# Attention, a PReLU layer pair and an expert mixture on one core: the second layer of ten expert pairs as seven block products, with the split weights kept in DRAM

## The chip, the cores and the metric

The kernel runs on 1 core of one Trainium2 chip. The metric is the device time of one execution in microseconds (us). Before the change the median of 3 runs is 849.52 us (847.73 to 849.97). The engines are TensorE (PE; its weight loads are listed apart as PEld), VectorE (DVE), ScalarE (ACT), GpSimd (POOL) and SyncE (SP), which only issues DMAs here.

## The reference, cut to what matters

```
attn = attention(q, k, v)             # local window of 16 plus block summaries; 2 x 8 heads x 768 x 64
x    = attn as 1536 tokens x 512
h    = x @ w_in                       # 512 x 2048
x    = (max(h, 0) + alpha * min(h, 0)) @ w_out
p    = domain_probs / (domain_probs.sum(-1) + 1e-9)
out  = 0
for e in range(4):                    # w1[e]: 512 x 1024, w2[e]: 1024 x 512
    h    = max(x @ w1[e], 0)
    out += p[:, e:e+1] * (h @ w2[e])
```

All of it is float32. The two batches of 768 tokens are worked on one after the other in the expert stage.

## The kernel before, in words

PE multiplies in the format fp32r. To keep float32 accuracy each operand is split into a high part (an ACT copy to fp32r) and a low part (a subtraction, value minus high part), and each product is three matmuls that add up in PSUM: high x high, high x low, low x high. Each matmul has its own weight load of 128 x 128.

The first two fifths of the span are attention and the PReLU layer, by an order written out by hand (`ORDER`) and then by unit (the loop over `units`). The expert stage follows (lines 726 to 749). It has 32 steps s: batch b = s // 16 and pair q = s % 16. A pair is 256 of the 4096 hidden columns, so four pairs make one expert.

*First layer of a step.* The 512 x 256 weight block and the 512 x 768 operand of a batch are cut into 2 x 2 blocks (256 x 128 of the weights, 256 x 384 tokens of the operand) and multiplied by seven block products instead of eight (Strassen's scheme in Winograd's form): `p1` to `p7` in `e_steps` (544). Each is 6 matmuls of 384 columns (2 row blocks x 3 terms). Results are combined by ACT copies (`keep`) and DVE sums, and `result` makes the high part `gh` (ACT, with the Relu) and the low part `gl` (DVE) of the hidden values. The sums of weights (S1 to S4) come from POOL (`e_sums`, 384), those of the operand (T1 to T4) from DVE (`x_combine`, 505).

*Second layer of a step.* `l2b` (612) takes six token tiles of 128. For each, 6 matmuls of 512 columns (2 row blocks x 3 terms) fill one PSUM bank, and DVE adds the bank, times the token's probability, to the accumulator `acc2`. The second layer of step s is carried out in step s + 1. The last tile of all goes in two halves of 256 columns (`l2b_last`, 596).

*Weights.* `e_prep(s)` (394) makes the split weights of step s, one step ahead. The raw weights come by DMA from SP into three slots tagged `raw`: `ra` for the first layer, `rb` for the second. ACT makes high parts and POOL low parts (`e_split`, 377), into rings of seven buffers. Both batches do this, so each pair is loaded and split twice.

*Order.* In the expert stage the order on PE and ACT is that of the program text (`manual_schedule`, 726): `p1`, the `p4` of the step before, `p2`, `p6`, the `p3` of the step before, `p5`, `p7`, and then the six `l2b` tiles with the pieces of `e_prep(s + 1)` merged in between. DVE, POOL and SP get their order from a planner that simulates the program. Each engine then takes its instructions strictly in order. In the steps 10 to 14 one piece each of the second batch's operand splits (`own1`) is merged in, in step 15 `late1`, in step 16 `last1`.

Of the kernel before, what the change touches and what calls it, by code (L numbers as in the profile page):

```python
# [16 lines left out]
B, H, S, D = 2, 8, 768, 64  # L17
P = 128
# [6 lines left out]
NAC = S // P  # L25
DM = H * D
KD = DM // P
FF1 = 2048
NE = 4
# [3 lines left out]
NFB = NF1 + NF2  # L33
G = 4
WBUFS = 7
MBUFS = 5
NG1 = NF1 // G
NQ = NF2 // 2
TP = S // 2
C0 = 256  # L40
CH = 512
NT = B * S // P

# [48 lines left out]
def kernel(  # L92
# [202 lines left out]
    ws, pw = {}, {}  # L295
# [74 lines left out]

    def e_load_b(s):
        q = s % NQ
        t = wp.tile([P, 2, DM], F32, tag="raw", name="rb", bufs=3)
        nc.sync.dma_start(out=t, in_=wb_in[1, 2 * q:2 * q + 2].rearrange("i p n -> p i n"))
        pw["b", s] = t

    def e_split(pool, k, src, n=DM):
        hi = pool.tile([P, n], F32R, tag="h", name=f"w{k}h")
        lo = pool.tile([P, n], F32R, tag="l", name=f"w{k}l")
        nc.scalar.activation(hi, src, AF.Copy)  # L380
        nc.gpsimd.tensor_tensor(lo, src, hi.bitcast(F32), op=ALU.subtract)  # L381
        return hi, lo

    def e_sums(s):
# [6 lines left out]
        nc.gpsimd.tensor_tensor(s34[:, 1], r[:, 2], s12[:, 1], op=ALU.subtract)  # L391
        pw["s", s] = s12, s34

    def e_prep(s):
        if s >= 2 * NQ:
            return []

        def part(names, src, pool=wpool[0]):
            hi, lo = e_split(pool, 0, src, len(names) * 2 * P)
            for i, name in enumerate(names):  # L400
                ws[s, name] = hi[:, i * 2 * P:(i + 1) * 2 * P], lo[:, i * 2 * P:(i + 1) * 2 * P]

        def flat(t):
            return t.rearrange("p a c -> p (a c)")

        steps = [
            lambda: part(("A11", "A12"), flat(pw["a", s][:, 1:3])),
            lambda: e_sums(s),
            lambda: part(("S1", "S2"), flat(pw["s", s][0])),
            lambda: part(("S3", "S4"), flat(pw["s", s][1])),  # L410
            lambda: part(("A22",), pw["a", s][:, 3], wa22),
        ]
        if s + 1 < 2 * NQ:
            steps.append(lambda: e_load_a(s + 1))
        for i in range(2):
            steps.append(lambda i=i: ws.__setitem__((s, i), e_split(wpool[1], 1, pw["b", s][:, i])))
        if s + 1 < 2 * NQ:
            steps.append(lambda: e_load_b(s + 1))
        return steps


    gs = {}
# [110 lines left out]
    def product(ps, s, b, aname, bname, first):  # L533
# [5 lines left out]
        for i, (l, r) in enumerate(terms):  # L539
            nc.tensor.matmul(  # L540
                ps, l, r, start=(first and i == 0), stop=(i == len(terms) - 1), skip_group_check=True
            )

    def e_steps(s):
        b = s // NQ
        v = {}

        def keep(name, ps):
            v[name] = gp.tile([P, TP], F32, tag="m", name=name, bufs=MBUFS)
            nc.scalar.activation(v[name], ps, AF.Copy)  # L550

        def result(f, half, src):
            gh = gp.tile([P, TP], F32R, tag="gh", name="gh")
            gl = gp.tile([P, TP], F32R, tag="gl", name="gl")
            gs[s, f, half] = gh, gl
            nc.scalar.activation(gh, src, AF.Relu)
            nc.vector.scalar_tensor_tensor(gl, src, 0.0, gh.bitcast(F32), op0=ALU.max, op1=ALU.subtract)

        def p1():
            v["b"] = ps_1.tile([P, TP], F32, tag="l1", name="cb")  # L560
            product(v["b"], s, b, "A11", "B11", True)
            keep("p1", v["b"])

        def p2():
            a = ps_w.tile([P, TP], F32, tag="w", name="ca")
            product(a, s, b, "A12", "B21", True)
            nc.vector.tensor_tensor(a, a, v["p1"], op=ALU.add)
            result(0, 0, a)

        def p6():  # L570
            product(v["b"], s, b, "S2", "T2", False)
            keep("u2", v["b"])

        def p5():
            v["d"] = ps_1.tile([P, TP], F32, tag="l1", name="cd")
            product(v["d"], s, b, "S1", "T1", True)

        def p7():
            product(v["b"], s, b, "S3", "T3", False)
            keep("u3", v["b"])  # L580
# [12 lines left out]

        return [p1, p2, p6, p5, p7, p4, p3]

    def l2b_last(s, i):

# [95 lines left out]
    for p in range(4 * G, 4 * G + 3):  # L693
        w_load(p)
    first.close()
    xe = ctx.enter_context(tc.tile_pool(name="xe", bufs=1))
    xeh = xe.tile([P, 3, 2, TP], F32R, name="xeh")
    xel = xe.tile([P, 3, 2, TP], F32R, name="xel")
    wa22 = ctx.enter_context(tc.tile_pool(name="wa22", bufs=2))
    ps_w = ctx.enter_context(tc.tile_pool(name="ps_w", bufs=2, space=PSUM))  # L700

    gp = ctx.enter_context(tc.tile_pool(name="gb", bufs=6))
    mbufs = MBUFS
    for f in (l1_minus, l1_prelu, l1_high, l1_low):
        f(G, 0, CH)
    for u, (n, c0, size) in enumerate(units):
# [17 lines left out]


    with tc.manual_schedule(engines={mybir.EngineType.PE, mybir.EngineType.Activation}):
        left = []
        l2 = l2_steps(len(units) - 1)[KD // 2:]
        for s in range(2 * NQ):
            p1, p2, p6, p5, p7, p4, p3 = e_steps(s)  # L730
            for f in [p1] + left[:1] + [p2, p6] + left[1:] + [p5, p7]:
                f()
            side = e_prep(s + 1)
            if NQ - 1 - len(own1) <= s < NQ - 1:
                side = side[:3] + [own1[s - NQ + 1 + len(own1)]] + side[3:]
            elif s == NQ - 1:
                side = late1 + side
            elif s == NQ:
                side = last1 + side
            keep = l2[-1:] if s == 2 * NQ - 1 else []  # L740
            merge(l2[:len(l2) - len(keep)], side)
            left = [p4, p3]
            l2 = [lambda i=i, s=s: l2b(s, i) for i in range(NAC)]
        for f in left + keep + l2[:-1]:
            f()
        l2b_last(2 * NQ - 1, NAC - 1)
# [59 lines left out]
```

## Time and profile before

| | |
|---|---|
| time of the runs | 849.52 us median, 847.73 to 849.97 |
| time of the profiled execution | 849.81 us |
| its span, first to last instruction | 848.0 us |
| granted TensorE clock, mean | 0.996 of full speed |
| DMA | 76.61 MB, mean 90 GB/s |
| HBM read / written | 72.63 MB / 3.15 MB |

The page of the profile gives the busy time of each engine, the chain of work that ended last, groups of instructions with their mean time, and DMA issues. A PE busy for 97% is not PE at its peak, since a matmul's duration in the records (0.39 us for 512 columns) is longer than the distance to the next start. So matmuls are read by their starts.

### The profile page before, as it was taken

To read this page: it belongs to the slowest core of one execution; us is meant where nothing else is said; L and a number is where in the kernel's file an instruction comes from. 1 tells how busy PE (TensorE), PEld (TensorE's weight loads), DVE (VectorE), ACT (ScalarE), POOL (GpSimd) and SP (SyncE) were. 2 spreads that over 40 slices of the span, in tenths; PEclk is the share of its full clock that TensorE was granted. 3 is DMA by queue.
4 is the path that set the end of the run, shared out by engine and by line. 5 is a ranking of instruction groups with operands and counts; after the bars stand their busy time and mean duration, and the time that the engine had idled before them with its cause. 6 is when DMAs were issued, how large, how long until landed. Compare 5 with 4: busy or idle time off the path is not lost.

```text
span 848.0 us, 12730 instructions
## 1 busy us (share of the span) xinstructions
PE 824.3 (97%) x4622; PEld 734.9 (87%) x4622; DVE 548.1 (65%) x1144; ACT 401.4 (47%) x988; POOL 326.8 (39%) x326
## 2 busy tenths in 40 slices
PE   4799999999999999999999999999999999999998
PEld 3689999888888888989889898898899899898997
DVE  7998767999983447455555576856555555545555
ACT  4999995544432324443433434534534434344340
POOL 0000000000022200475675676765766756756630
PEclk9899999999999999999999999999999999999999
DMA  8999412333320000113122122122322131121201
GB/s 303 286 307 295 147 44 76 100 99 100 100 75 25 26 1 0 50 51 100 51 67 83 50 73 77 50 77 72 125 84 66 50 99 51 57 93 50 75 1 75
DMA packets 39695, 76.61 MB, mean 90 GB/s; under 512 B 3792, under 2 KB 15568, under 8 KB 39632
## 3 DMA queue, kind: packets, MB, share of 16 engines
q1 hardware_dynamic: 39056, 75.51, 28.2%
q8 instruction: 36, 0.59, 0.3%
q10 hardware_dynamic: 576, 0.28, 0.1%
q14 instruction: 27, 0.22, 0.1%
HBM read 72.63 MB, written 3.15 MB: 89 GB/s over the span
## 4 chain that ended last, share of the span: by engine, by line
PE 86%; DVE 7%; DMA 3%; ACT 2%; issue 0%; SPq 0%; ACTq 0%
PE l L428 58%; PE cb L540 15%; PE cd L540 7%; PE ca L540 4%; DVE acc L519 1%; DVE acc L626 1%; DMA vcat<-in_vw 1%; PE s L212 1%; PE xps L274 1%; ACT sm L231 1%; DVE sm L222 1%; DMA kv<-in_vt 1%; DVE vs L176 1%; DMA raw<-in_wa 1%; PE pt L256 1%; DMA mask<-in_mask 1%
## 5 line engine op out<-in xcount | busy, mean ns | idle before, releaser
L381 POOL TENSOR_TENSOR w0l<-ra,w0h 128x512 fp32r<-128x512 f32 (+1 forms) x64 | 70.4, 1100 | 349.9 <-ACT w0h L380 349.9
L626 DVE SCALAR_TENSOR_TENSOR acc<-l,prob_sb,acc 128x512 f32<-128x512 f32 x179 | 133.8, 750 | 74.6 <-PE l L428 74.6
L428 PE MATMUL l<-w1h,gh 128*128 128x512 f32 (+1 forms) x386 | 149.8, 388 | 1.1 <-DVE acc L626 1.1
L428 PE MATMUL l<-w1h,gl 128*128 128x512 f32 (+1 forms) x386 | 150.4, 390 | 0.0
L428 PE MATMUL l<-w1l,gh 128*128 128x512 f32 (+1 forms) x386 | 150.3, 389 | 0.0
L381 POOL TENSOR_TENSOR w0l<-s,w0h 128x512 fp32r<-128x512 f32 x64 | 85.6, 1357 | 2.9 <-ACT w0h L380 2.9
L381 POOL TENSOR_TENSOR w1l<-rb,w1h 128x512 fp32r<-128x512 f32 x64 | 81.9, 1301 | 11.9 <-ACT w1h L380 11.9
L428 PEld LDWEIGHTS l<-w1h,gh 128*128 128x128 f32 x386 | 72.5, 188 | 15.8 <-DVE acc L626 1.6
L428 PEld LDWEIGHTS l<-w1h,gl 128*128 128x128 f32 x386 | 72.4, 188 | 15.0
L428 PEld LDWEIGHTS l<-w1l,gh 128*128 128x128 f32 x386 | 72.4, 188 | 14.4
L428 PE MATMUL l<-xh,w0h 128*128 128x512 f32 (+1 forms) x240 | 84.5, 352 | 0.0
L428 PE MATMUL l<-gh,w1h 128*128 128x512 f32 (+1 forms) x240 | 83.3, 350 | 0.0
L428 PE MATMUL l<-xl,w0h 128*128 128x512 f32 (+1 forms) x240 | 83.1, 346 | 0.0
L428 PE MATMUL l<-xh,w0l 128*128 128x512 f32 (+1 forms) x240 | 83.1, 346 | 0.0
L428 PE MATMUL l<-gh,w1l 128*128 128x512 f32 (+1 forms) x240 | 82.9, 347 | 0.0
L550 ACT ACTIVATE p<-cb 128x384 f32<-128x384 f32 x32 | 15.7, 492 | 140.3 <-PE cb L540 140.3
L428 PE MATMUL l<-gl,w1h 128*128 128x512 f32 (+1 forms) x240 | 81.4, 347 | 0.0
L388 POOL TENSOR_TENSOR s<-ra 128x256 f32<-128x256 f32 x32 | 23.6, 738 | 125.6 <-DMA ra<-in_wb 121.7
L540 PE MATMUL cb<-xeh,w0h 128*128 128x384 f32 x192 | 64.4, 335 | 0.2
L540 PE MATMUL cb<-xeh,w0l 128*128 128x384 f32 x192 | 64.2, 334 | 0.0
L540 PE MATMUL cb<-xel,w0h 128*128 128x384 f32 x192 | 64.2, 334 | 0.0
L453 DVE SCALAR_TENSOR_TENSOR l<-m,beta,l 128x512 f32<-128x512 f32 (+1 forms) x60 | 38.6, 644 | 23.8 <-ACT m L447 23.7
(104 smaller groups left out, 1836.4 us busy)
## 6 DMA issues: line engine op xcount, KB each, us to landing
raw<-in_wa SPq DMA_DIRECT2D x32, 512.0 KB, 3.8
ra<-in_wb SPq DMA_DIRECT2D x64, 256.0 KB, 3.0
rb<-in_wb SPq DMA_DIRECT2D x32, 512.0 KB, 3.6
q<-in_qh SPq DMA_DIRECT2D x24, 256.0 KB, 5.3
kw<-in_kw SPq DMA_DIRECT2D x24, 192.0 KB, 5.5
vcat<-in_vw SPq DMA_DIRECT2D x12, 384.0 KB, 6.3
kv<-in_kt SPq DMA_DIRECT2D x8, 384.0 KB, 5.7
kv<-in_vt SPq DMA_DIRECT2D x8, 384.0 KB, 6.0
```

The lines of the kernel that those rows point to most:

```text
L176: nc.vector.tensor_reduce(vs[:, hp, KW:NK], st.pop(("v", b, hp)), axis=AX.X, op=ALU.add)
L212: nc.tensor.matmul(sp[:, u], q[:, u // 2, u % 2], kw[:, :, u // 2, u % 2], start=True, stop=True)
L222: nc.vector.tensor_tensor_reduce(sm[:, u], sp[:, u], mask[:, m], -1.0 / math.sqrt(D), 3.0e38, ALU.add, ALU.min, mx[:, u:u + 1],)
L231: nc.scalar.activation(sm[:, u], sm[:, u], AF.Exp, bias=mx[:, u:u + 1], scale=-1.0, accum_out=sume[:, u:u + 1],)
L256: nc.tensor.transpose(pt[0:NK, u], pp[:, u], ident)
L381: nc.gpsimd.tensor_tensor(lo, src, hi.bitcast(F32), op=ALU.subtract)
L388: nc.gpsimd.tensor_tensor(s12[:, 0], r[:, 0], r[:, 3], op=ALU.add)
L428: ins = nc.tensor.matmul(ps, a, c, start=(i == 0), stop=(i == n - 1))
L453: nc.vector.scalar_tensor_tensor(ps, m, beta[:, i:i + 1], ps, op0=ALU.mult, op1=ALU.add)
L540: nc.tensor.matmul(ps, l, r, start=(first and i == 0), stop=(i == len(terms) - 1), skip_group_check=True)
L550: nc.scalar.activation(v[name], ps, AF.Copy)
L626: nc.vector.scalar_tensor_tensor(acc2[:, t], ps, pe, acc2[:, t], op0=ALU.mult, op1=ALU.add)
```

## The change

- For the five pairs of steps (18, 19) to (26, 27), all in the second batch, the second layers of two steps are done together. 768 tokens x 512 hidden columns times 512 x 512 weights are cut into 2 x 2 blocks, and seven block products take the place of eight (`l2_quad`). Each is 3 token tiles x 6 matmuls of 256 columns. DVE adds each finished half bank to one or two blocks of the accumulator. These products are mixed into the first-layer products of the following steps by a pattern (`paired`), in which a dot stands for one group of 6 matmuls.
- The sums of hidden values that this needs are made on DVE (`s_sums`), from float32 copies of the Relu results that ACT writes (`field`), and split by ACT and POOL (`s_split`).
- The sums of weights (T1 to T4) for these pairs are made on DVE in the first batch (`t_sums`), split by ACT and DVE (`t_split`) and written to DRAM.
- In the first batch every split weight is also written to DRAM (`put`). In the second batch nothing is split any more; the parts are read back (`e_fetch`, `b_load`).
- `rb` of odd steps gets a buffer of its own; the ring of first-layer copies shrinks from 5 to 4; the operand splits of the second batch (`own1`) move to steps 12 to 14.

```diff
-MBUFS = 5
+MBUFS = 4
+UA, UB = NQ + 2, 2 * NQ - 4
...
     def e_load_b(s):
         q = s % NQ
-        t = wp.tile([P, 2, DM], F32, tag="raw", name="rb", bufs=3)
+        if s % 2:
+            t = gp.tile([P, 2, DM], F32, tag="rb", name="rb", bufs=1)
+        else:
+            t = wp.tile([P, 2, DM], F32, tag="raw", name="rb", bufs=3)
...
+    def put(dst, pair):
+        for h, t in enumerate(pair):
+            nc.sync.dma_start(out=dst[:, h], in_=t.bitcast(F32))
...
+    def t_place(i):
+        k, c = 2 * (i % 2), S + 2 * P * (1 + i // 2)
+        return slice(None), slice(k, k + 2), slice(c, c + 2 * P)
+
+    def t_view(s, i):
+        d = 2 * P * (i in (1, 2))
+        return pw["b", s - i % 2][:, :, d:d + 2 * P]
+
+    def t_sums(s):
+        t1, t2, t3, t4 = (t_view(s, i) for i in range(4))
+        for y, p, q in ((t1, t3, t1), (t3, t2, t3), (t2, t2, t1), (t4, t4, t2)):
+            nc.vector.tensor_tensor(y, p, q, op=ALU.subtract)
+
+    def t_split(s, i):
+        t, hi, lo = t_view(s, i), xh[t_place(i)], xl[t_place(i)]
+        nc.scalar.activation(hi, t, AF.Copy)
+        nc.vector.tensor_tensor(lo, t, hi.bitcast(F32), op=ALU.subtract)
+        put(dt[unit(s), i], (hi, lo))
...
     def e_prep(s):
         if s >= 2 * NQ:
             return []
+        if s >= NQ:
+            return [lambda: e_fetch(s)]
 
         def part(names, src, pool=wpool[0]):
...
+            pair = e_split(pool, 0, src, len(names) * 2 * P)
+            named(s, names, *pair)
+            put(da[s, names[0]], pair)
+
+        def second(i):
+            ws[s, i] = e_split(wpool[1], 1, pw["b", s][:, i])
+            put(dw[s, i], ws[s, i])
...
+        if s % 2 and quad(s + NQ):
+            steps.append(lambda: t_sums(s))
+        elif s % 2 == 0 and quad(s - 1 + NQ):
+            for i in range(4):
+                steps.insert(2 * i + 1, lambda i=i: t_split(s - 1, i))
         return steps
...
         def result(f, half, src):
+            if quad(s):
+                name = f"A{half + 1}{2 - s % 2}"
+                if name == "A21":
+                    nc.scalar.activation(field(s, name, f), src, AF.Relu)
+                    return
...
+            if quad(s):
+                nc.scalar.activation(field(s, name, f), src, AF.Relu)
...
+    def s_sums(s, f):
+        a11, a12, a21, a22 = (field(s, n, f) for n in ("A11", "A12", "A21", "A22"))
+        nc.vector.tensor_tensor(a22, a21, a22, op=ALU.add)
+        nc.vector.tensor_tensor(a21, a11, a21, op=ALU.subtract)
+        nc.vector.tensor_tensor(a11, a22, a11, op=ALU.subtract)
+        nc.vector.tensor_tensor(a12, a12, a11, op=ALU.subtract)
+
+    def s_split(s, k, f):
+        src, c = field(s, ("A22", "A11", "A12", "A21")[k], f), slice(f * TP, (f + 1) * TP)
+        nc.scalar.activation(xh[:, k, c], src, AF.Copy)
+        nc.gpsimd.tensor_tensor(xl[:, k, c], src, xh[:, k, c].bitcast(F32), op=ALU.subtract)
+
+    def l2_quad(a):
...
+        plan = (
+            ("B21", base(a, 0), 0, True, ((0, 0),)),
+            ("T4", base(a, 1), 1, True, ((1, 0),)),
+            ("B11", base(a + 1, 0), 0, True, ((0, 0),)),
+            ("T1", summed(0), 1, False, ((1, 1),)),
+            ("T2", summed(1), 0, False, ((0, 1),)),
+            ("B22", summed(2), 1, False, ((0, 1),)),
+            ("T3", summed(3), 0, False, ((1, 0), (1, 1))),
+        )
+
+        def go(k, i):
...
+            ps = u[i][:, part]
+            (bh, bl), terms = bs[n, bname], []
+            for f in range(2):
+                gh, gl = left(f, 0, i), left(f, 1, i)
+                terms += [(gh, bh[:, f]), (gh, bl[:, f]), (gl, bh[:, f])]
...
+            for half, d in to:
+                t = NAC + half * (NAC // 2) + i
+                dst = acc2[:, t, d * 2 * P:(d + 1) * 2 * P]
+                nc.vector.scalar_tensor_tensor(dst, ps, prob_sb[:, t, e:e + 1], dst, op0=ALU.mult, op1=ALU.add)
+            if i == NAC // 2 - 1 and a + 2 < UB:
+                b_load(n + 1, bname)
...
+        own_at = {NQ - 4: own1[:2], NQ - 3: own1[2:4], NQ - 2: own1[4:], NQ - 1: late1, NQ: last1}
...
+                paired(a, "1.2.6.5.7..4.3" if n == 7 else "1.2.6..5.7..4..3.", old[done:13], splits)
+                paired(a + 1, "1.2..6..5.7..4..3.", old[13:] + q[:3])
...
+        paired(UB, "1..2..6...5..7...4...3...", old[done:], splits)
```

## Rows read from the trace of the kernel before

**Rows 1.** The page, busy us, share of the span, instructions of each engine:
```profile
PE 824.3 (97%) x4622; PEld 734.9 (87%) x4622; DVE 548.1 (65%) x1144; ACT 401.4 (47%) x988; POOL 326.8 (39%) x326
```

**Rows 2.** Waits of PE, 300 us to the end: us in total, times, longest:
```profile
PE l L428 <- DVE acc L626: 1.1, 1, 1.1
```

**Rows 3.** Windows by step: us, then busy time per engine, clock, DMA share, GB/s:
```profile
451.19:466.70 15.51, 15.51 (x80) 14.06 (x79) 8.29 (x13) 6.28 (x13) 9.99 (x10) 1.00 0.22 69
...
497.71:513.88 16.17, 16.05 (x80) 13.97 (x79) 13.90 (x18) 7.02 (x14) 10.83 (x10) 1.00 0.21 65
545.59:561.09 15.50, 15.50 (x79) 14.05 (x79) 9.36 (x15) 6.69 (x14) 10.84 (x12) 1.00 0.22 69
576.60:593.55 16.95, 15.80 (x79) 13.98 (x79) 11.89 (x17) 7.94 (x17) 9.92 (x11) 1.00 0.18 62
```

**Rows 4.** The chain of waits, one step: start us, us, what:
```profile
609.06 8.20 PE l L428 x36
617.26 2.10 PE cb L540 x12
624.57 8.20 PE l L428 x36
```

**Rows 5.** Timeline of PE at the end: start us, us, engine, line, operation:
```profile
843.14 0.28 PE L428 MATMUL l<-w1h,gh 128*128 128x256 f32 x1
...
844.45 0.28 PE L428 MATMUL l<-w1h,gl 128*128 128x256 f32 x1
```

**Rows 6.** The chain of waits in the first stage, 125 to 127 us:
```profile
125.28 2.04 PE l L428 x17
```

**Rows 7.** Groups of DVE, whole span: count | busy us, mean ns | idle before:
```profile
L626 DVE SCALAR_TENSOR_TENSOR acc<-l,prob_sb,acc 128x512 f32<-128x512 f32 x179 | 133.8, 750 | 74.6 <-PE l L428 74.6
...
L341 DVE TENSOR_TENSOR t<-t,e 128x512 f32<-128x512 f32 x32 | 21.7, 682 | 0.1
...
L591 DVE TENSOR_TENSOR cd<-cd,u 128x384 f32<-128x384 f32 x32 | 18.1, 566 | 9.9 <-PE cd L540 9.9
...
L609 DVE SCALAR_TENSOR_TENSOR acc<-l,prob_sb,acc 128x256 f32<-128x256 f32 x2 | 1.0, 483 | 0.2 <-PE l L428 0.2
```

**Rows 8.** Groups of ACT and of POOL, 600 to 800 us:
```profile
L380 ACT ACTIVATE w1h<-rb 128x512 fp32r<-128x512 f32 x26 | 14.8, 615 | 0.0
...
L556 ACT ACTIVATE gh<-cd 128x384 fp32r<-128x384 f32 x13 | 6.4, 491 | 15.7 <-DVE cd L591 15.7
...
L381 POOL TENSOR_TENSOR w0l<-ra,w0h 128x512 fp32r<-128x512 f32 x13 | 19.0, 1460 | 18.1 <-ACT w0h L380 18.1
...
L381 POOL TENSOR_TENSOR w0l<-ra,w0h 128x256 fp32r<-128x256 f32 x13 | 9.6, 739 | 0.0
```

**Rows 9.** Timelines of DVE and of POOL, 576 to 594 us:
```profile
579.16 1.02 DVE L501 TENSOR_TENSOR xel<-acc,xeh 128x384 fp32r<-128x384 f32 x2
...
580.76 3.11 DVE L501 TENSOR_TENSOR xel<-acc,xeh 128x384 fp32r<-128x384 f32 x2
...
580.59 1.30 POOL L381 TENSOR_TENSOR w0l<-ra,w0h 128x512 fp32r<-128x512 f32 x1 [3.05 <-ACT w0h L380]
```

**Rows 10.** Timeline of POOL, end of one step's work and its gap:
```profile
458.15 2.54 POOL L381 TENSOR_TENSOR w1l<-rb,w1h 128x512 fp32r<-128x512 f32 x2
464.56 0.74 POOL L388 TENSOR_TENSOR s<-ra 128x256 f32<-128x256 f32 x1 [3.87 <-DMA ra<-in_wb]
```

**Rows 11.** Windows of attention's loads and of the last output writes, columns as above:
```profile
20.00:60.00 40.00, 34.67 (x319) 30.80 (x320) 38.60 (x157) 38.11 (x142) 0.00 (x0) 0.91 1.00 308
...
838.00:844.00 6.00, 6.00 (x32) 5.10 (x31) 3.56 (x5) 0.00 (x0) 0.00 (x0) 1.00 0.41 158
```

**Rows 12.** Timeline of SP's queue, one load of raw weights:
```profile
445.23 0.34 SPq L367 DMA_DIRECT2D ra<-in_wb  x1
445.61 0.56 SPq L368 DMA_DIRECT2D ra<-in_wb  x1
```

More of the change, by code (lines that the diff above doesn't have):

```diff
@@ L392, in e_sums, with quad, unit, get @@
         pw["s", s] = s12, s34
+    def quad(s):
+        return UA <= s < UB
+    def unit(s):
+        return (s - UA % NQ) // 2
+    def put(dst, pair):
+        for h, t in enumerate(pair):
+            nc.sync.dma_start(out=dst[:, h], in_=t.bitcast(F32))
+    def get(pool, src, n=DM):
+        hi = pool.tile([P, n], F32R, tag="h", name="wfh")
+        lo = pool.tile([P, n], F32R, tag="l", name="wfl")
+        for h, t in enumerate((hi, lo)):
+            nc.sync.dma_start(out=t.bitcast(F32), in_=src(h))
+        return hi, lo
@@ new lines, in b_load @@
+    def b_load(j, name):
+        half = slice(0, 2 * P) if name in ("B11", "B21") else slice(2 * P, DM)
+        hi = wpool[1].tile([P, 2, 2 * P], F32R, tag="h", name="bh")
+        lo = wpool[1].tile([P, 2, 2 * P], F32R, tag="l", name="bl")
+        for h, t in enumerate((hi, lo)):
+            if name[0] == "T":
+                nc.sync.dma_start(out=t.bitcast(F32), in_=dt[j, int(name[1]) - 1][:, h])
+            else:
+                for f in range(2):
+                    a = UA % NQ + 2 * j + 2 - int(name[1])
+                    nc.sync.dma_start(out=t[:, f].bitcast(F32), in_=dw[a, f][:, h, half])
+        bs[j, name] = hi, lo
@@ new lines, with named, e_fetch @@
+    PARTS = (("A11", "A12"), ("S1", "S2"), ("S3", "S4"), ("A22",))
+    def named(s, names, hi, lo):
+        for i, name in enumerate(names):
+            ws[s, name] = hi[:, i * 2 * P:(i + 1) * 2 * P], lo[:, i * 2 * P:(i + 1) * 2 * P]
+    def e_fetch(s):
+        q = s % NQ
+        for names in PARTS:
+            n = len(names) * 2 * P
+            pool = wpool[0] if len(names) > 1 else wa22
+            named(s, names, *get(pool, lambda h: da[q, names[0]][:, h], n))
+        if not quad(s):
+            for f in range(2):
+                ws[s, f] = get(wpool[1], lambda h: dw[q, f][:, h])
@@ L396, in e_prep @@
             return []
+        if s >= NQ:
+            return [lambda: e_fetch(s)]
         def part(names, src, pool=wpool[0]):
-            hi, lo = e_split(pool, 0, src, len(names) * 2 * P)
-            for i, name in enumerate(names):
-                ws[s, name] = hi[:, i * 2 * P:(i + 1) * 2 * P], lo[:, i * 2 * P:(i + 1) * 2 * P]
+            pair = e_split(pool, 0, src, len(names) * 2 * P)
[4 more added lines that the diff above has]
+            put(dw[s, i], ws[s, i])
         def flat(t):
@@ L412, in e_prep @@
         ]
-        if s + 1 < 2 * NQ:
+        if s + 1 < NQ:
             steps.append(lambda: e_load_a(s + 1))
         for i in range(2):
-            steps.append(lambda i=i: ws.__setitem__((s, i), e_split(wpool[1], 1, pw["b", s][:, i])))
-        if s + 1 < 2 * NQ:
+            steps.append(lambda i=i: second(i))
+        if s + 1 < NQ:
             steps.append(lambda: e_load_b(s + 1))
+        if s % 2 and quad(s + NQ):
[3 more added lines that the diff above has]
+                steps.insert(2 * i + 1, lambda i=i: t_split(s - 1, i))
         return steps
@@ L542, in product, with field @@
             )
+    bs, fs = {}, {}
+    def field(s, name, f):
+        if name == "A12":
+            j = (s - UA) // 2
+            if (j, name) not in fs:
+                fs[j, name] = wp.tile([P, 2, TP], F32, tag="raw", name="a12", bufs=3)
+            return fs[j, name][:, f]
+        k = 2 * ("A22", "A11", "A21").index(name) + f
+        return acc[:, k * TP:(k + 1) * TP]
     def e_steps(s):
@@ new lines, in l2_quad, with base, summed @@
+    def l2_quad(a):
+        n, u = (a - UA) // 2, {}
+        def base(s, half):
+            return lambda f, h, i: gs[s, f, half][h][:, i * P:(i + 1) * P]
+        def summed(k):
+            return lambda f, h, i: (xh, xl)[h][:, k, f * TP + i * P:f * TP + (i + 1) * P]
+        plan = (
[8 more added lines that the diff above has]
+        def go(k, i):
+            bname, left, part, first, to = plan[k]
+            if k == 0:
+                u[i] = ps_2.tile([P, 2, 2 * P], F32, tag="l2", name="l2q")
+            ps = u[i][:, part]
+            (bh, bl), terms = bs[n, bname], []
+            for f in range(2):
+                gh, gl = left(f, 0, i), left(f, 1, i)
+                terms += [(gh, bh[:, f]), (gh, bl[:, f]), (gl, bh[:, f])]
+            for j, (l, r) in enumerate(terms):
+                nc.tensor.matmul(
+                    ps, l, r, start=(first and j == 0), stop=(j == len(terms) - 1), skip_group_check=True
+                )
+            e = a % NQ * NE // NQ
+            for half, d in to:
[4 more added lines that the diff above has]
+                b_load(n + 1, bname)
+        return [lambda k=k, i=i: go(k, i) for k in range(len(plan)) for i in range(NAC // 2)]
@@ L695 @@
     first.close()
+    dr = ctx.enter_context(tc.tile_pool(name="dr", bufs=1, space=bass.MemoryType.DRAM))
+    da, dw, dt = {}, {}, {}
+    for q in range(NQ):
+        for names in PARTS:
+            da[q, names[0]] = dr.tile([P, 2, len(names) * 2 * P], F32, name=f"da{q}{names[0]}")
+        for f in range(2):
+            dw[q, f] = dr.tile([P, 2, DM], F32, name=f"dw{q}{f}")
+    for j in range((UB - UA) // 2):
+        for i in range(4):
+            dt[j, i] = dr.tile([P, 2, 2, 2 * P], F32, name=f"dt{j}{i}")
     xe = ctx.enter_context(tc.tile_pool(name="xe", bufs=1))
@@ L726, with standard @@
     with tc.manual_schedule(engines={mybir.EngineType.PE, mybir.EngineType.Activation}):
-        left = []
+        left, keep = [], []
         l2 = l2_steps(len(units) - 1)[KD // 2:]
-        for s in range(2 * NQ):
+        own_at = {NQ - 4: own1[:2], NQ - 3: own1[2:4], NQ - 2: own1[4:], NQ - 1: late1, NQ: last1}
+        def standard(s, l2, left):
             p1, p2, p6, p5, p7, p4, p3 = e_steps(s)
+            if not left:
+                left, l2 = l2[:2], l2[2:]
             for f in [p1] + left[:1] + [p2, p6] + left[1:] + [p5, p7]:
@@ L733 @@
             side = e_prep(s + 1)
[L734 to L739, printed above, removed]
+            if s in own_at:
+                side = side[:3] + own_at[s] + side[3:]
             keep = l2[-1:] if s == 2 * NQ - 1 else []
             merge(l2[:len(l2) - len(keep)], side)
-            left = [p4, p3]
@@ L743, with paired @@
-            l2 = [lambda i=i, s=s: l2b(s, i) for i in range(NAC)]
+            return [lambda i=i, s=s: l2b(s, i) for i in range(NAC)], [p4, p3], keep
+        def paired(s, order, fill, after=()):
+            fill, after = iter(fill), iter(after)
+            steps = dict(zip("1265743", e_steps(s)))
+            e_prep(s + 1)[0]()
+            for x in order:
+                if x == ".":
+                    next(fill)()
+                    next(after, lambda: None)()
+                    continue
+                steps[x]()
+                if s % 2 and quad(s) and x in "43":
+                    s_sums(s, int(x == "4"))
@@ new lines @@
+        for s in range(UA):
+            l2, left, _ = standard(s, l2, left)
+        for name in ("B21", "T4", "B11"):
+            b_load(0, name)
+        old = None
+        for a in range(UA, UB, 2):
+            q = l2_quad(a)
+            if old is None:
+                paired(a, "1.26.57...4...3", left + l2)
+                for name in ("T1", "T2", "B22", "T3"):
+                    b_load(0, name)
+                paired(a + 1, "1.2.6.57..4.3", q[:6])
+                k = 6
+            else:
+                splits = [lambda k=k, f=f, s=a - 1: s_split(s, k, f) for k in range(4) for f in (1, 0)][1:]
+                n = 13 - done
+                paired(a, "1.2.6.5.7..4.3" if n == 7 else "1.2.6..5.7..4..3.", old[done:13], splits)
+                paired(a + 1, "1.2..6..5.7..4..3.", old[13:] + q[:3])
+                k = 3
+            s_split(a + 1, 0, 1)
+            old, done = q, k
@@ L744 @@
+        splits = [lambda k=k, f=f, s=UB - 1: s_split(s, k, f) for k in range(4) for f in (1, 0)][1:]
+        paired(UB, "1..2..6...5..7...4...3...", old[done:], splits)
+        l2, left = [lambda i=i: l2b(UB, i) for i in range(NAC)], []
+        for s in range(UB + 1, 2 * NQ):
+            l2, left, keep = standard(s, l2, left)
         for f in left + keep + l2[:-1]:
```

## The prediction, made before the changed kernel was run

> **What bounds the kernel now.** I read the busy shares first. PE (TensorE) is busy for 97% of the span, the next engine, DVE, for 65%, and ACT and POOL for less than half [rows 1]. The list of waits says the same of the stretch this change touches: from 300 us to the end PE waited once, for 1.1 us [rows 2]. So only two things move the time here: the columns that PE has to stream, and new waits of PE.
>
> Then I cut the expert stage into its 32 steps by time. An undisturbed step takes 15.50 to 15.51 us with PE busy throughout, DVE 8.29, ACT 6.28 and POOL about 10 [rows 3]. The chain of waits shows what a step consists of: 36 second-layer matmuls of 512 columns in 8.20 us, and until the next such block 7.31 us for the 42 product matmuls of 384 columns, the first twelve in 2.10 [rows 4]. That is 0.228 and 0.174 us each. Twelve second-layer matmuls of 256 columns stand at the very end: from the first start to the last, 843.14 to 844.45, are 11 spacings of 0.119 us [rows 5]; seventeen in the first stage take 2.04 us, 0.120 each [rows 6]. Their weight loads of 0.19 us overlap and do not set this spacing. I take 0.1195 us.
>
> **Part 1, PE columns.** Ten steps (18 to 27) become five pairs. Before, a pair's second layer is 72 matmuls x 0.228 = 16.40 us. After, it is 7 products x 3 token tiles x 2 row blocks x 3 terms = 126 matmuls of 256 columns, 126 x 0.1195 = 15.06 us. The saving is 1.34 us a pair, 6.7 us for five. The first-layer products are unchanged. An eighth fewer columns buys only 8% because each matmul has a fixed part: 128 columns more cost 0.054 us (0.228 against 0.174), so 512 would be 0.215, and 0.013 is left, which 126 matmuls pay instead of 72.
>
> The Trainium skill (TensorE: Matmul & The Clock Gate, Back-to-back issue gap) gives the isolated spacing as columns / 2.4 GHz plus about 2.5 ns. By that the pair would go from 15.5 to 13.8 us and the saving would be an estimated 8.9 us. The rows have some 11 ns more in each matmul, so the sum goes by the rows.
>
> **Part 2, DVE in the first batch.** In five odd steps t_sums adds four subtractions of 512 columns, both inputs in SBUF, and in the next step t_split adds four more, and four ACT copies of 0.615 us [rows 8], which fit into ACT's 9 idle us. A subtraction of that shape takes 0.682 us on DVE while POOL rests [rows 7]. Beside a busy POOL it is another matter: two 384-column subtractions started at 579.16 took 1.02 us while POOL was idle, and two started at 580.76, with POOL at work from 580.59, took 3.11 us [rows 9]. So one costs 0.51 free and 1.55 contended, about 1.04 more, near one POOL operation of 1.3. Scaled, a 512-column one is 0.68 to 1.72 us.
>
> The Trainium skill (SBUF — State Buffer, Who interferes with whom) calls the port pair of VectorE and GpSimd an exclusive lock: a VectorE instruction with two SBUF inputs waits until the GpSimd instruction that got it first has ended. The trace agrees, 0.51 against 1.55 us each. Without that rule t_split would be four times 0.68 in DVE's idle time and cost nothing; with it, it is a term.
>
> t_split runs in the second-layer window, where POOL is in its low parts: 4 x 1.72 = 6.9 us more on DVE. What such an addition does to PE three steps show: one with 1.07 us more on DVE kept its 15.50, one with 5.6 more (13.90) took 16.17, one with 3.6 more took 16.95, because the two contended subtractions there stood between two evictions [rows 3]. Per step the price is thus between 0 and 1.45 us, and it may be more for 512 columns; the nearest in size is 0.66. I take 0.5, since ACT's copies space the four out: 5 x 0.5 = 2.5 us, bounds 0 and 7.3. t_sums overwrites the raw weights, so it waits for POOL's last low part, about 9.5 us after the window's start, and meets POOL's gap of 3.87 us [rows 10]: 4 x 0.68 = 2.7 us, between the rows with 0 and 0.66. I take 0.3: 1.5 us, bounds 0 and 7.3. Behind a waiting t_sums on DVE's in-order queue stand the result sums; behind them, on ACT, the copies that PE's last product waits for.
>
> **Part 3, the batch change.** The second batch's splits move. Step 15 loses its POOL work, since its weights now come ready from DRAM. Its 1.45 us stall came from contended splits; uncontended, four take 2.0 instead of 4.1 us, and I leave 0.25: minus 1.2, bounds minus 1.45 and 0. Steps 10 to 14 lose two stalls of about 0.66 us and steps 12 to 14 get the same subtractions in three steps: plus 0.3, bounds minus 0.7 and plus 1.5. The smaller ring of first-layer copies (four for five) costs nothing as long as a step's four have three free ones to choose from, which the order of the products gives; a copy forced to wait for the third product would add about 0.15 us a step, 2.7 us in 18 steps.
>
> **Part 4, dependences in the pairs.** DVE gives up 12 evictions of 0.750 us and gets 24 of 0.483 [rows 7], eight sums of 0.51 to 1.55, and six low parts instead of eight: some 23 to 26 us in 29.65, where it was 16.6 in 31. POOL falls to eight low parts, so the lock is mostly gone. Each eviction must be over before the next product writes the same bank; at least two other groups (1.4 us) stand between, against 0.48 us of work. The chain into the summed operands (DVE 0.57, ACT Relu 0.49, DVE 0.51, ACT copy 0.49, a POOL low part between 0.74 and 1.46 [rows 7, 8], and handovers: some 3.5 us) has 6 us of PE work in front of its first reader. I take 0.1 us in each of ten steps: 1.0, bounds 0 and 6.6 (0.66 each).
>
> **Part 5, DMA.** A first-batch step writes 2.88 MB beside 1.05 MB read; with t_split another 2.10 MB every second step. Two steps then move 9.96 MB in 31.0 us, 321 GB/s. Before, the saturated attention stretch reached 308 GB/s of reads at a share of 1.00, and the output writes 158 GB/s at 0.41, or 385 at a full share [rows 11]. By these 2.10 / 308 + 7.86 / 385 = 27.2 us: it fits in 31, at 88%. At 308 for everything it is 32.3 us, 1.3 us of lag a pair, 6.6 in all; the seven buffers hold more than a step's work ahead. I count 0 for it, bounds 0 and 14. In the pairs 7.34 MB of reads in 29.65 us are 248 GB/s, 80%, fetched a whole step ahead. SP issues some 19 DMAs a step at 0.34 to 0.56 us [rows 12], 8 of 15.5 us.
>
> **Sum.** Minus 6.7, minus 1.2, plus 0.3, 2.5, 1.5 and 1.0 is minus 2.6 us. The profiled execution took 849.81 us for a span of 848.0; it becomes 847.2. It lay 0.3 above the median of 849.52, so the median becomes 846.9.
>
> **Rivals.**
> - Everything added stays hidden. For it: DVE has 7 idle us in a step, and 1.07 us more cost nothing. Against: the steps with 16.17 and 16.95. Minus 6.7 and minus 1.2: 841.6.
> - DVE's in-order queue eats the gain. If t_sums is queued ahead of evictions while POOL still works, or a pair of splits falls between two evictions, each of the ten steps pays as the rows did: at 0.66 the sum is about 0, 849.3; at 1.45 it is plus 8, 857. It is slower from about 0.9 us a step. For it: both rows of before. Against: POOL's gap after its last low part.
> - DMA saturates, the one that surely ends slower. If the mix of writes and reads gets 270 GB/s, a pair of steps needs 36.9 us; five fall behind by 29 us, some 15 of which the buffers swallow: plus 14, about 861. It decides from below 321 GB/s. For it: no row shows writes under load, and some of these move 1 KB pieces. Against: the 385 of the outputs.
> - The change doesn't do what it says: the weight loads bind at 256 columns. The 0.119 us spacing speaks against it; it would give about 850.
>
> **How the numbers follow.** Forecast 0.45, all hidden 0.20, DVE queue 0.20, DMA 0.13, weight loads 0.02. A measurement of this kernel tells about 0.3%, 2.5 us, from no change: faster is under 847.0, slower over 852.1. The forecast case spans 843.5 to 850 and gives 0.25 faster and 0.20 same. All hidden is faster. The DVE case is 0.12 same and 0.08 slower, DMA slower, weight loads same: faster 0.45, same 0.34, slower 0.21. The range reaches to the all-hidden case and to the middle of the DVE case, 841.5 to 854.0.
>
> **What would show it.** In the trace after, a pair's second layer should be 126 matmuls at 0.119 to 0.120 us, and an undisturbed pair should repeat after 29.7 us. Steps 3 to 12 should alternate near 15.8 and 16.0 us, with contended subtractions of 1.5 to 1.8 us and DVE as PE's releaser. Step 15 should fall under 16 us. The DMA share should stay under 0.95 in those steps. The prediction is wrong if PE waits on DMA or on a POOL tile in the first batch, or if a step there exceeds 17 us.

## The result, and the profile after

The changed kernel takes 853.74 us (median of 7 runs, 851.89 to 855.29); the kernel before, run beside it, 849.69 (847.73 to 850.31). The ratio is 1.0051, 95% interval 1.0036 to 1.0066: slower by half a per cent, where 846.9 and faster was forecast. The profiled execution took 852.68 us for a span of 850.8, so the two profiled executions differ by 2.87 us and their spans by 2.8, where the medians differ by 4.05. The accounts below go by the spans.

The page after, busy us, share of the span and instructions of each engine [rows 1]:

```profile
PE 821.4 (97%) x4892; PEld 743.9 (87%) x4892; DVE 607.0 (71%) x1274; ACT 397.6 (47%) x982; POOL 218.3 (26%) x206
```

PE has less to do, DVE 59 us more, POOL 109 us less. The waits of PE from 330 to 600 us (us in total, times, longest) show that PE is no longer undisturbed [rows 2]:

```profile
PE cb L620 <- ACT w0h L384: 2.3, 1, 2.3
PE l L508 <- DVE acc L778: 2.2, 4, 0.8
PE cd L620 <- DVE gl L653: 1.8, 2, 1.3
PE cb L620 <- POOL w0l L385: 0.7, 1, 0.7
```

The list names 7.0 us in all; some of the lost time stands in it as busy time, so I went by starts. For each group of six matmuls I took the distance to the next group's start and subtracted its streaming time (0.228, 0.174 or 0.119 us a matmul). What is left over, summed, is called lost time here. From 330 us it is 3.0 us before and 12.6 us after, an estimate good to some 0.3 us, and nearly all of it after lies in four places.

*The border of steps 0 and 1: 5.15 us.* Before, PE went from step 0's last product to 24 leftover matmuls of the PReLU layer and from there to step 1's first product. The chain of waits of before shows it (start us, us, what):

```profile
344.32 1.05 PE cb L540 x6
345.37 5.48 PE l L428 x24
350.85 2.10 PE cb L540 x12
```

After, those 24 stand earlier, among the products of step 0, and after its last product PE has nothing but step 1. The timeline of PE after (start us, us, engine, line, operation, idle before and what ended it):

```profile
350.19 0.34 PE L620 MATMUL cb<-xeh,w0l 128*128 128x384 f32 x1
352.83 0.44 PE L620 MATMUL cb<-xh,w0h 128*128 128x384 f32 x1 [2.31 <-ACT w0h L384]
353.11 0.34 PE L620 MATMUL cb<-xl,w0h 128*128 128x384 f32 x1
354.19 0.69 PE L620 MATMUL cb<-xh,w0l 128*128 128x384 f32 x1 [0.74 <-POOL w0l L385]
354.68 0.52 PE L620 MATMUL cb<-xh,w0h 128*128 128x384 f32 x1
355.00 0.52 PE L620 MATMUL cb<-xl,w0h 128*128 128x384 f32 x1
```

PE waits for ACT's high part of step 1's weights, then for POOL's low part, and then runs for a while at 0.32 us a matmul instead of 0.174. Against the streaming time the first three groups lose 2.47, 1.76 and 0.88 us; the slower spacing is some 1.3 us of that (nine matmuls at 0.32). The first ACT copy of step 1's weights is late in neither kernel relative to the products: it starts 1.55 us after the start of step 0's last copy of `u` in both (timelines of ACT, first before, then after):

```profile
345.46 0.49 ACT L550 ACTIVATE u<-cb 128x384 f32<-128x384 f32 x1 [2.07 <-PE cb L540]
346.58 0.53 ACT L556 ACTIVATE gh<-c 128x384 fp32r<-128x384 f32 x1 [0.62 <-DVE c L582]
347.01 0.62 ACT L380 ACTIVATE w0h<-ra 128x512 fp32r<-128x512 f32 x1
```
```profile
350.62 0.49 ACT L641 ACTIVATE u<-cb 128x384 f32<-128x384 f32 x1 [4.22 <-PE cb L620]
351.74 0.52 ACT L652 ACTIVATE gh<-c 128x384 fp32r<-128x384 f32 x1 [0.62 <-DVE c L680]
352.17 0.61 ACT L384 ACTIVATE w0h<-ra 128x512 fp32r<-128x512 f32 x1
```

What is gone is the 5.48 us of PE work that covered it.

*The five steps with `t_split`: 3.5 us* (0.22, 1.04, 0.61, 0.96 and 0.67). As in the prediction, a step is called odd or even here by the step whose weights it prepares; its number elsewhere is that of its products. Windows of an odd step (first line) and of the step after it (second), columns as in [rows 3]:

```profile
409.72:425.23 15.51, 15.51 (x80) 14.06 (x79) 9.56 (x14) 6.62 (x13) 13.27 (x14) 1.00 1.00 344
425.23:441.80 16.57, 15.82 (x80) 14.00 (x79) 14.89 (x21) 8.42 (x18) 9.21 (x6) 1.00 0.85 299
```

The odd step, in which `t_sums` begins, loses nothing. In the other DVE has 14.89 us of work. The timeline of DVE there (L426 is `t_sums`, L431 `t_split`):

```profile
425.82 0.68 DVE L426 TENSOR_TENSOR rb<-rb 128x512 f32<-128x512 f32 x1
...
428.61 0.74 DVE L778 SCALAR_TENSOR_TENSOR acc<-l,prob_sb,acc 128x512 f32<-128x512 f32 x1
429.27 2.83 DVE L431 TENSOR_TENSOR xl<-rb,xh 128x512 fp32r<-128x512 f32 x2
432.03 0.74 DVE L778 SCALAR_TENSOR_TENSOR acc<-l,prob_sb,acc 128x512 f32<-128x512 f32 x1
432.70 1.09 DVE L431 TENSOR_TENSOR xl<-rb,xh 128x512 fp32r<-128x512 f32 x1
433.71 0.74 DVE L778 SCALAR_TENSOR_TENSOR acc<-l,prob_sb,acc 128x512 f32<-128x512 f32 x1
434.38 1.81 DVE L431 TENSOR_TENSOR xl<-rb,xh 128x512 fp32r<-128x512 f32 x1
```

The reader is to see two low parts in a row (2.83 us) between two evictions. They hold up the next eviction, and PE waits for its bank. One subtraction of 512 columns is 0.68 us while POOL rests and 1.1 to 1.8 beside it. Two of the four sums of `t_sums` run in this window too, ahead of the evictions. In the first of the five split steps all four were over before the window, and it is the one that loses only 0.22 us.

*The operand splits of the second batch (`own1`): 3.14 us* (1.98 and 1.16 in steps 12 and 13; the first of them takes 17.5 us). *The first second-layer product of the first pair: 1.11 us.* Of before, 1.34 us of operand splits and step 15's 1.43 us are gone.

The pairs themselves came as computed. The chain of waits after, start of the same product in two pairs that follow each other:

```profile
678.13 1.43 PE l2q L735 x12
...
707.72 1.43 PE l2q L735 x12
```

That is 0.119 us a matmul and 29.59 us a pair (15.16 and 14.43 by the first-layer products), 1.43 less than 2 x 15.51. Five are 7.2 us. The account is then 5.15 + 3.5 + (3.14 - 1.34) + 1.11 - 1.43 - 7.2 = plus 2.9 us, against a span of plus 2.8.

### The profile page after: what moved, and what is told of

Its sections match the earlier page's. It is cut to its first block, busy times and chain, and to the rows that moved or that the text cites. A ratio compares the mean times of both kernels' runs of the same rounds, so it can differ in the third digit from the quotient of the medians.

```text
span 850.8 us, 14131 instructions
## 1 busy us (share of the span) xinstructions
PE 821.4 (97%) x4892; PEld 743.9 (87%) x4892; DVE 607.0 (71%) x1274; ACT 397.6 (47%) x982; POOL 218.3 (26%) x206
## 4 chain that ended last, share of the span: by engine, by line
PE 70%; DVE 10%; DMA 8%; issue 7%; POOL 2%; ACT 2%; SPq 2%; ACTq 0%; POOLq 0%; DVEq 0%
PE l L508 40%; PE cb L620 11%; PE l2q L735 8%; PE cd L620 5%; PE ca L620 3%; DVE acc L778 2%; DMA raw<-in_wa 2%; DVE xl L431 2%; DMA dw<-w1l 2%; DMA ra<-in_wb 1%; DVE acc L599 1%; PE xps L275 1%; PE s L213 1%; PE pt L257 1%; SPq L406 1%
## 5 line engine op out<-in xcount | busy, mean ns | idle before, releaser
L778 DVE SCALAR_TENSOR_TENSOR acc<-l,prob_sb,acc 128x512 f32<-128x512 f32 x119 | 88.2, 746 | 34.1 <-PE l L508 34.1
L508 PE MATMUL l<-w1h,gh 128*128 128x512 f32 x192 | 75.2, 392 | 2.2 <-DVE acc L778 2.2
L508 PE MATMUL l<-w1h,gl 128*128 128x512 f32 x192 | 75.0, 391 | 0.0
L508 PE MATMUL l<-w1l,gh 128*128 128x512 f32 x192 | 75.0, 391 | 0.0
L742 DVE SCALAR_TENSOR_TENSOR acc<-l2q,prob_sb,acc 128x256 f32<-128x256 f32 x120 | 54.3, 477 | 21.8 <-PE l2q L735 20.9
L527 ACT ACTIVATE m<-l 128x512 f32<-128x512 f32 (+1 forms) x60 | 30.6, 512 | 46.5 <-PE l L508 46.2
L508 PEld LDWEIGHTS l<-xh,w0h 128*128 128x128 f32 x240 | 45.4, 189 | 5.9
L508 PEld LDWEIGHTS l<-gh,w1h 128*128 128x128 f32 x240 | 45.4, 189 | 5.6
L508 PEld LDWEIGHTS l<-gh,w1l 128*128 128x128 f32 x240 | 45.4, 189 | 5.6
L508 PEld LDWEIGHTS l<-gl,w1h 128*128 128x128 f32 x240 | 45.4, 189 | 5.6
L508 PEld LDWEIGHTS l<-xh,w0l 128*128 128x128 f32 x240 | 45.3, 189 | 5.7
```

Source lines behind the costliest of these rows:

```text
L508: ins = nc.tensor.matmul(ps, a, c, start=(i == 0), stop=(i == n - 1))
L527: nc.scalar.activation(m, gs[i, c0][0], AF.Relu, scale=-1.0)
L742: nc.vector.scalar_tensor_tensor(dst, ps, prob_sb[:, t, e:e + 1], dst, op0=ALU.mult, op1=ALU.add)
```

## The experiments

In the order below, the expectations call them e1_step0, e2_before_order, e3_low_on_pool, e5_dram_only, e6_double_t, e4_own_order, e7_spread and e8_spread_own. Each was timed in turn with the kernel before on its chip (849.10 us for e1 to e4, 849.73 for e5 to e8); the ratio is to that, with its 95% interval.

**The border of steps 0 and 1.** The line that moves the leftovers is in `standard`; it is part of the change, though the diff ahead of the prediction leaves it out. `left` holds `p4` and `p3` of the step before, and is empty in step 0 and behind the pairs.

```diff
         def standard(s, l2, left):
             p1, p2, p6, p5, p7, p4, p3 = e_steps(s)
-            if not left:
+            if not left and s:
                 left, l2 = l2[:2], l2[2:]
```

> Changed kernel, but in the first expert step the two leftover groups of the PReLU layer's second product (24 matmuls of 512 columns, 5.5 us) stay behind the step's products, as in the kernel before, instead of being moved between them. Theory 'lost cover': in the trace of the changed kernel PE loses 2.47 + 1.76 + 0.88 us at the border of steps 0 and 1, since nothing is left for it to do while ACT and POOL split the weights of step 1. Then 5.1 us come back: about 848.6 us, 0.1% below the kernel before. Rival 'late writes': step 1's split weights come late because ring buffers wait to be written to DRAM. Then at least 4 of the 5 us stay: 853 us.

Measured: 848.90 us (846.90 to 851.02), ratio 0.9987 (0.9971 to 1.0003). The chain of waits has the old order back, and PE runs through:

```profile
343.90 1.05 PE cb L620 x6
344.95 5.48 PE l L508 x24
350.43 2.10 PE cb L620 x12
```

The lost time falls to 8.1 us; nothing at the border is left, 3.96 are in the split steps, 3.26 in the operand splits, 1.11 in the first pair. The counter-test gives the kernel before those two lines and nothing else:

```diff
+            if not left:
+                left, l2 = l2[:2], l2[2:]
```

> Kernel before with only this order of the leftover groups in step 0; no DRAM copies, no block products in the second layer. 'Lost cover': plus 5.1 us, about 854.8. 'Late writes': no change, 849.7, since nothing is written to DRAM here.

Measured: 854.10 us (853.41 to 856.09), ratio 1.0053 (1.0036 to 1.0069), plus 5.0 us. Its waits of PE from 330 us on:

```profile
PE cb L540 <- ACT w0h L380: 2.3, 1, 2.3
PE l L428 <- DVE acc L626: 1.1, 1, 1.1
PE cb L540 <- POOL w0l L381: 0.7, 1, 0.7
```

The first and the last are those of the changed kernel, to the tenth. So the two lines alone explain the changed kernel's distance from a tie, and without them the rest of the change neither wins nor loses measurably.

**What holds the split steps.** All below have the first edit. If DVE's contended subtractions are the price, the low parts of T1 to T4 might go to POOL itself:

```diff
     def t_split(s, i):
...
-        nc.vector.tensor_tensor(lo, t, hi.bitcast(F32), op=ALU.subtract)
+        nc.gpsimd.tensor_tensor(lo, t, hi.bitcast(F32), op=ALU.subtract)
```

> As e1_step0, and the four low parts of the weight sums T1 to T4 (t_split) are subtracted on POOL instead of DVE. Theory 'port lock': the five split steps lose 0.22, 1.04, 0.61, 0.96 and 0.67 us, 3.5 in all, because DVE's subtractions with two SBUF inputs wait for POOL's and hold up the evictions. Without them on DVE these steps fall to under 0.1 us each: about 845.1 us. Rival 'DMA': they lose it because the DMA engines are saturated there; then nothing changes, 848.6. Rival 'POOL too long': POOL gets 4 x 1.1 us more, the sums S1 to S4 come late and PE waits for them: over 850.

Measured: 862.92 us (858.98 to 863.47), ratio 1.0130 (1.0091 to 1.0169): a miss. The split windows fell to between 0.12 and 0.29 us of lost time each, but the products of the odd steps lost 1.9 to 4.2 us, and 8.3 where the operand splits come in. PE waits there for copies that stand behind weight copies on ACT. Waits of PE (first line), then of ACT, 380 to 570 us:

```profile
PE cb L620 <- ACT p L641: 10.1, 5, 2.4
```
```profile
ACT w0h L384 <- POOL s L393: 17.5, 5, 3.5
...
ACT w0h L384 <- DMA ra<-in_wb: 9.7, 3, 3.4
...
ACT w0h L384 <- DMA da6A<-w0l: 2.8, 1, 2.8
```

POOL's sums come too late, raw weights too, and twice (2.8 us here, 2.6 once more) split weights had not yet been written out when a buffer was wanted. So the four subtractions on DVE are where the split windows' price comes from, and POOL has no room to take them. Whether they cost it by their wait for POOL or by their mere number is not shown: this edit takes away both.

To see whether the DRAM round trip costs anything by itself, T1 to T4 and the pairs go:

```diff
     def quad(s):
-        return UA <= s < UB
+        return False
...
-        for s in range(UA):
-            l2, left, _ = standard(s, l2, left)
...
-        for s in range(UB + 1, 2 * NQ):
+        for s in range(2 * NQ):
             l2, left, keep = standard(s, l2, left)
```

> As e1_step0 without any pair: all second layers as before, no T1 to T4, all split weights written to DRAM in the first batch and read back in the second. PE has 6.7 us more columns, and loses neither the 3.9 us of the split steps nor the 1.1 us in the first pair: 848.9 + 1.7 = 850.6 us if the operand splits lose what they lose in e1_step0; 849.3 if they lose less because DMA is not saturated. If DRAM writing by itself costs PE something, it is over 851.

Measured: 848.11 us (846.72 to 849.14), ratio 0.9980 (0.9971 to 0.9990). Lost time is 1.4 us in all, 1.2 of it operand splits; no step loses to DMA. An undisturbed stretch of one step's length in the first batch, columns as in [rows 3]:

```profile
413.50:429.00 15.50, 15.50 (x80) 14.05 (x79) 8.29 (x13) 6.33 (x14) 10.05 (x10) 1.00 0.72 254
```

Writing and reading back all split weights thus costs PE nothing and brings step 15's 1.4 us. Beside the first experiment, 848.1 against 848.9 us and 1.4 against 8.1 of lost time, it says that the pairs with T1 to T4 cost about as much as their 7.2 us.

How far DMA is from its limit was asked by writing T1 to T4 twice, the second time to DRAM that nobody reads:

```diff
         put(dt[unit(s), i], (hi, lo))
+        put(dx[unit(s), i], (hi, lo))
```

> As e1_step0, and T1 to T4 are written to DRAM twice, the second time to a place that nobody reads: 12.06 MB instead of 9.96 in two steps. The highest rate in the trace of the changed kernel is 345 to 362 GB/s at a share of 1.0, 10.7 to 11.2 MB in 31 us. If DMA is just enough there, this exceeds it by about 1 MB, 3 us in each of five pairs of steps, and after some 10 us of slack PE waits: 852 to 858 us. If DMA is far from the limit, no change: 848.9.

Measured: 877.91 us (874.38 to 880.14), ratio 1.0329 (1.0299 to 1.0359), far above what was expected. ACT's longest waits are for raw weights (380 to 590 us; the window is of the same kernel):

```profile
ACT w0h L384 <- DMA ra<-in_wb: 23.3, 5, 6.2
```
```profile
437.00:455.60 18.60, 18.60 (x96) 16.94 (x96) 12.32 (x18) 5.58 (x11) 7.41 (x8) 1.00 0.97 323
```

Against the first experiment 2.10 MB more every second step cost 29.0 us, 5.8 for each of the five, which is the time that 2.10 MB take at 362 GB/s, the highest rate in a window of the changed kernel. Almost nothing of it was hidden, so the changed kernel stood right at the limit.

**Two ways to lay the DVE work.** `own1` holds the splits of the blocks B11, B21 and B22 and then eight subtractions, which need B11 split first. Here the three come one a step, B11 last:

```diff
-own_at = {NQ - 4: own1[:2], NQ - 3: own1[2:4], NQ - 2: own1[4:], NQ - 1: late1, NQ: last1}
+own_at = {NQ - 4: own1[2:3], NQ - 3: own1[1:2], NQ - 2: own1[:1], NQ - 1: own1[3:] + late1, NQ: last1}
```

> As e1_step0, and the operand splits of the second batch are spread as B22, B21, B11 over steps 12 to 14, with the eight subtractions for T1 to T3 in step 15, in which POOL has nothing to do. In the changed kernel steps 12 to 15 lose 1.98 + 1.16 + 0 us. 'Port lock': the subtractions cost 0.5 instead of 1.0 to 1.6 us each and these steps lose 0.7 together: about 846.2 us. Rival 'amount': what counts is DVE's work in one window, not POOL; then step 15 with 7 us more loses at least 2 us: 848.6 or more.

Measured: 848.60 us (846.18 to 850.26), ratio 0.9983 (0.9968 to 0.9997), no different from the first experiment. Steps 12 and 13 lose nothing, but DVE gets all eight subtractions behind B11 in step 14, while POOL still works, and that one loses 4.06 us (window over the step and what lies around it):

```profile
564.00:583.60 19.60, 17.64 (x79) 15.35 (x79) 16.50 (x23) 7.34 (x15) 8.83 (x6) 0.91 0.88 299
```

As they did not run in step 15, beside a resting POOL, the run does not tell POOL's part from the mere amount. What it does show is that the price moves to the second-layer window in which the DVE work meets. So the T splits were spread: two of the four in the window, the other two among the products of the next step, where DVE idles.

```diff
-            for i in range(4):
-                steps.insert(2 * i + 1, lambda i=i: t_split(s - 1, i))
+            for i in (1, 3):
+                steps.insert(2 * i - 1, lambda i=i: t_split(s - 1, i))
+            pend[s] = [lambda i=i: t_split(s - 1, i) for i in (0, 2)]
...
-            for f in [p1] + left[:1] + [p2, p6] + left[1:] + [p5, p7]:
+            for f in [p1] + left[:1] + [p2, p6] + left[1:] + [p5] + pend.pop(s, []) + [p7]:
```

> As e1_step0, and of the four splits of T1 to T4 two stay in the second-layer window and two move behind the fifth product of the next step, where POOL rests and DVE has 3 idle us. Theory 'DVE late in one window': the five split steps lose 3.9 us in e1_step0, because four contended subtractions stand between the evictions; with two they fall under 0.3 us each: about 846.5 us. Rival 'ring and DMA': the writes go out later and the ring buffers are late as in e3_low_on_pool; then ACT waits for a DMA and the time is 850 or more.

Measured: 847.94 us (846.49 to 851.21), ratio 0.9984 (0.9971 to 0.9997). All five split steps take 15.51 us, as expected. But one of the two splits that were put off (T1) lies across the part of `xl` into which B11 is split, and is now written out too late for it. The timeline of DVE in step 12:

```profile
536.62 3.24 DVE L584 TENSOR_TENSOR xl<-acc,xh 128x768 fp32r<-128x768 f32 x2 [1.83 <-DMA dt<-xl]
539.79 0.74 DVE L781 SCALAR_TENSOR_TENSOR acc<-l,prob_sb,acc 128x512 f32<-128x512 f32 x1
540.45 3.68 DVE L602 TENSOR_TENSOR acc<-acc 128x384 f32<-128x384 f32 x3
```

DVE waits 1.83 us for the write-out, the operand splits and subtractions come in a heap behind it, steps 12 and 13 lose 5.7 and 1.0 us, and the gain is gone. The last one combines both: one piece a step, first B21, whose place the early two splits leave, then B11, so that the subtractions fall into two windows by four.

```diff
-own_at = {NQ - 4: own1[:2], NQ - 3: own1[2:4], NQ - 2: own1[4:], NQ - 1: late1, NQ: last1}
+own_at = {NQ - 4: own1[1:2], NQ - 3: own1[:1], NQ - 2: own1[2:3], NQ - 1: own1[3:] + late1, NQ: last1}
```

> As e7_spread, and the operand splits of the second batch in the order B21, B11, B22 over steps 12 to 14 (in e4_own_order all eight subtractions ran in one window, since they became ready with the last of the three), so that four of the eight subtractions are ready after B11 and four after B22, in different steps. 'DVE late in one window': the steps 12 to 15 lose 3.3 us in e1_step0 and 1.3 as in the kernel before here: about 844.6 us. Rival 'DMA': DMA is behind from step 11 on, POOL's work comes late and these steps lose 3 us in any order: 846.5.

Measured: 843.60 us (841.38 to 844.27), ratio 0.9932 (0.9912 to 0.9951). It beats both kernels. Lost time is 2.45 us, 1.1 of it the first pair. A split step and its DVE (window, then timeline):

```profile
413.00:428.50 15.50, 15.50 (x80) 14.05 (x79) 12.13 (x19) 7.76 (x17) 10.96 (x10) 1.00 0.88 322
```
```profile
422.79 1.13 DVE L433 TENSOR_TENSOR xl<-rb,xh 128x512 fp32r<-128x512 f32 x1
423.84 0.74 DVE L781 SCALAR_TENSOR_TENSOR acc<-l,prob_sb,acc 128x512 f32<-128x512 f32 x1
424.50 1.13 DVE L433 TENSOR_TENSOR xl<-rb,xh 128x512 fp32r<-128x512 f32 x1
425.55 2.07 DVE L781 SCALAR_TENSOR_TENSOR acc<-l,prob_sb,acc 128x512 f32<-128x512 f32 x3
```

One low part and one eviction are 1.87 us of DVE, in which PE fills 1.4 banks (1.37 us each); DVE catches up with the three evictions behind. Two low parts and an eviction were 3.57 us, 2.6 banks.

## Why the prediction was wrong

- **The step that failed is one that was not there.** The working goes through five parts and has no term for the border of steps 0 and 1. It read `paired` and the memory traffic closely and passed over the line in `standard`, which was written for the step behind the pairs and fires in step 0 too. Its cost could be read from the trace of before: 5.48 us of PE work stood over the first splits of step 1. With 5.1 us more the sum would have been 852.0 for the median. The first two experiments show this cause from both sides: without the line the 5.15 us are gone and the distance to the kernel before goes from plus 4.05 to minus 0.20 us; the line alone costs 5.0. Two of the prediction's own signs of being wrong came true: a wait of PE on a POOL tile in the first batch (0.7 us at this border) and a step there of over 17 us (step 12 with 17.5, by the operand splits). The upper end of its range, 854.0, was set by a busier DVE queue; that 853.74 lies below it is luck.
- **Columns** (minus 6.7): right, minus 7.2. The pair was to repeat after 29.7 us and does after 29.59. By the isolated spacing that the Trainium skill (TensorE: Matmul & The Clock Gate, Back-to-back issue gap) gives, its second layer would be 126 x 0.109 = an estimated 13.8 us; the starts give 126 x 0.119 = 15.0. The measured one decides.
- **`t_split` and `t_sums`** (2.5 and 1.5): 3.5 together, near their sum of 4.0. The odd steps were to be near 15.8 and are at 15.51: two of DVE's sums found room among the products there, the other two run in the split steps, so how the 3.5 divides was not told apart. The place and the mechanism, two low parts of 1.1 to 1.8 us between two evictions, are the ones named; with the low parts on POOL the price left the split windows. How much of it is the wait for POOL stays open.
- **Operand splits** (plus 0.3, at most 1.5): mis-sized, plus 1.8. Three steps for the work of five put more DVE work into one window, and the two last experiments, 847.94 and 843.60, differ in the order of these splits alone.
- **Step 15** (minus 1.2) and **dependences in the pairs** (plus 1.0): right, minus 1.43 and plus 1.11, though the latter is one stall in the first pair and not a tenth in each step. DVE's load of a pair was added up wrongly: 16.6 less 9.0 plus 11.6, plus eight sums of 0.51 to 1.55, less two low parts of 0.56 are 22 to 30 us and not 23 to 26; the window of the pair from 678.13 has 21.41.
- **DMA** (0): right for PE, but not by the margin given. The odd steps from 3 on were to stay under a share of 0.95; the one shown above has 1.00, and two more are:

```profile
473.40:488.90 15.50, 15.50 (x80) 14.06 (x79) 9.57 (x14) 6.55 (x13) 13.23 (x14) 1.00 1.02 341
505.40:520.90 15.50, 15.50 (x80) 14.05 (x79) 9.54 (x15) 6.68 (x13) 13.28 (x14) 1.00 1.02 345
```

  POOL's waits for raw weights are no sign of this by themselves: from 380 to 570 us there are five, 28.9 us in all, where the kernel before has twelve, 46.2 us, at a share of 0.22. What changes is when the wait ends. In step 12 (its first 15.50 us, then a line of POOL's timeline):

```profile
537.10:552.60 15.50, 14.18 (x71) 12.42 (x70) 13.68 (x16) 6.85 (x13) 14.30 (x13) 1.00 1.03 362
538.30 0.74 POOL L392 TENSOR_TENSOR s<-ra 128x256 f32<-128x256 f32 x1 [5.62 <-DMA ra<-in_wb]
```

  POOL begins its sums 1.2 us into the second-layer window; before, it began them 2.1 us ahead of one (464.56 against 466.70 [rows 3, 10]). With the DRAM writes of the split weights alone, at a share of 0.72, it still began 2.8 us ahead (415.89 against 418.65), so the lateness comes with T1 to T4. That makes POOL late into step 12, where it meets the operand splits. How much of their 1.8 us is due to it was not told apart.
- **The median.** The step-by-step account closes for the spans, at plus 2.9. The medians differ by 4.05; the profiled execution was one of the changed kernel's shorter ones, and what the others lose more stays open.

## What to carry to other kernels

When a line of the order is rewritten for a new case, evaluate it for every step that passes through it, the first and the last above all, and ask of each moved block of PE work what preparation it stood over: here its length, 5.48 us, was nearly the price, 5.15. Stalls behind an in-order queue go by how much meets between two evictions, so the same DVE work costs nothing one piece at a time and 0.2 to 1.0 us a step two at a time. A transfer that only just fits shows no wait on PE; here the share in the windows (1.00 to 1.03) and the later start of POOL's sums showed it, and a run with more to transfer measured it.

## What the runs showed of the hardware

- Reads and writes of DRAM together reached 341 to 362 GB/s at a DMA share of 1.00 to 1.03, where reads alone gave 308 at 1.00 [rows 11]. The 385 worked out for writes was too high for the mix (with it the prediction's 9.96 MB in 27.2 us are 366).
- After 2.3 us of idle time PE ran at the lower of its two clock levels, 1.2 and 2.4 GHz, for a while: 0.32 us for 384 columns, which is 1.2 GHz, where 0.174 is the usual. The granted clock of this window is a mean over both:

```profile
352.80:358.80 6.00, 5.23 (x19) 4.91 (x20) 0.55 (x2) 3.35 (x7) 5.94 (x6) 0.72 0.85 318
```

- A 512-column subtraction of two operands in SBUF took 0.68 us on DVE with POOL at rest and up to 1.81 beside it, and POOL's own low parts of 512 columns grew as well: two in 3.42 us, against 2.54 [rows 10]. The Trainium skill (SBUF — State Buffer, Who interferes with whom) says that the loser of the port pair waits for the whole of the other's instruction; the trace agrees, on both engines.
